# A decode attention and gated-MLP kernel: each V tile by one transfer of 128 partitions in place of four of 32

## The chip, the cores and the metric

The kernel runs on one core of one Trainium2 chip. The metric is the device time of one execution in microseconds (us). Three runs of the kernel before gave 198.82, 197.82 and 198.64 us, a median of 198.64 us. The profile comes from one more execution, which took 197.94 us.

A core has five engines that run their own instruction streams: PE (TensorE, matmul), DVE (VectorE), ACT (ScalarE), POOL (GpSimd) and SP (SyncE). Data comes from device memory (HBM) into the on-chip memory (SBUF, 128 partitions) by DMA transfers. A transfer is issued from the stream of SP, ACT or POOL; the profile counts 16 DMA engines that move the bytes, whichever stream issued it.

## The reference, cut to what matters

One decode step for 8 sequences (batch B = 8, one query each), 32 query heads over 8 key/value heads, a head size of 128, and a window of the last 2048 of 8192 cached keys. Beside the attention stands a gated MLP whose output, after a SiLU, multiplies the attention output.

```python
xn = layernorm(x)                                        # x: [8, 1, 512]
q  = (xn @ wq)                                           # wq: [512, 4096] -> 32 heads of 128
k, v = k_cache[:, :, Sk-W:, :], v_cache[:, :, Sk-W:, :]  # [8, 8, 2048, 128] of [8, 8, 8192, 128]
p  = softmax(q k^T / sqrt(128));  s = (p v) @ wo         # four query heads share a key/value head
h  = sigmoid(xn @ w_gate) * (xn @ w_up)                  # [512, 1792] each
g  = silu(h @ w_down)                                    # [1792, 512]
out = x + s * g
```

All inputs and the output are bf16. The bytes read are 33.6 MB of K, 33.6 MB of V and about 14 MB of weights.

## The kernel before, in words

Everything large goes through a ring of five SBUF buffers (`RING = 5`, `ring_tile` in line 109). The order of the tiles is: `wq`, eight K tiles, eight V tiles (one for each sequence), gate and up weights, down weights, and `wo`. A tile may be loaded as soon as the tile five places before it has been used up; `issue_loads` (line 190) issues what is allowed at each step of the main loop. `wq` and K are issued on SP's queue, V and the later weights on POOL's (`load_v` in line 137, `load_gate_up`, `load_down` and `load_wo` in lines 153 to 179). Every large transfer's instruction has line 107.

A K tile is 4 MB: 32 pairs of (sequence, head) outside, four runs of 128 keys inside, so 128 partitions of 32 KB each, in one transfer. A V tile is also 4 MB: one sequence, eight heads, 16 runs of 128 consecutive keys, again 128 partitions of 32 KB. Before the change it comes in four transfers of 1 MB. Transfer `s` fills partitions 32s to 32s+31 with four of the 16 runs; inside it the eight heads stand outside and the four runs inside, so partition 32s + 4h + i holds head h, run 4s + i. They are issued in the order `V_ORDER = (0, 2, 1, 3)`: partitions 0 to 31, 64 to 95, 32 to 63, 96 to 127.

The work is a software pipeline written out by hand. The main loop (line 620) has 122 steps. Step t turns one eighth of a K tile on DVE (`k_turn`, line 437), multiplies an earlier one with the queries on PE (`qk`, line 452), and from step 58 on also multiplies an eighth of a V tile with the probabilities (`pv`, line 570). A K tile counts as used up after its last `qk`, a V tile after its last `pv`. The sequences come in two halves of four (`hb`); for each half the softmax follows its fourth K tile: row maximum (`soft_max_part`, line 466), exponentials on ACT (`soft_exp`, line 480), 32x32 turns on DVE (`soft_turn`, line 500), and then `soft_spread` (line 513).

`soft_spread` multiplies the turned probabilities by a constant matrix of zeros and ones, `spread`, so that each probability lands in the partition that holds its keys in the V tile. `soft_mask` (line 532) then multiplies by `Hm`, which is one where a partition holds head h and zero elsewhere, so that one matmul over 128 partitions serves all eight heads. Both constants are made once, from the identity matrix: `Hm` by one reduction on DVE (line 278), `spread` by a memset and four copies on POOL (lines 286 and 291). They hold the order of the partitions in the V tile.

After the last V tile follow the MLP (`unit_in`, `unit_mid`, `unit_out`), the output projection with `wo` (line 666, in six pieces so that the last one is small), and two small stores.

Of the kernel before, what the change touches and what calls it, by code (L numbers as in the profile page):

```python
# [10 lines left out]
def kernel(  # L11
# [13 lines left out]
    nc = tc.nc  # L25
    P = 128
    B, _, D = A_x.shape
    _, Hkv, Sk, Dh = A_k_cache.shape
# [6 lines left out]
    win0 = Sk - W  # L35
# [7 lines left out]
    PP = P // Hkv  # L43
    CH = W // PP
# [23 lines left out]
    CB = CH // 4  # L68
    NCH = 2
    RING = 5  # L70
    VI = 32 // Hkv
    VS = PP // VI
    V_ORDER = (0, 2, 1, 3)
    NCOL = 2
    DC = D // NCOL

    bf16 = mybir.dt.bfloat16
    f32 = mybir.dt.float32
    AF = mybir.ActivationFunctionType
    ALU = mybir.AluOpType  # L80
    AX = mybir.AxisListType
# [3 lines left out]
    consts = ctx.enter_context(tc.tile_pool(name="consts", bufs=1))  # L85
# [18 lines left out]
    def load(dst, src, q=None):  # L104
        if q is None:
            q = nc.sync
        q.dma_start(out=dst, in_=src)  # L107

    def ring_tile(shape, name):
        return ring.tile(shape, bf16, name=name, tag="ring", align_bytes=ALIGN)  # L110

    x_bf = work.tile([B, D], bf16, name="x_bf")
    for c in range(4):
        nc.scalar.dma_start(
            out=x_bf[:, P * c : P * (c + 1)],
            in_=A_x.flatten_outer_dims()[:, P * c : P * (c + 1)],
# [19 lines left out]

    def load_v(b):
        t = ring_tile([P, CH, Dh], "v_sb")
        for s in V_ORDER:
            k0 = win0 + VI * CH * s  # L140
            load(
                t[32 * s : 32 * (s + 1)].rearrange("p c d -> p (c d)"),
                A_v_cache[b, :, k0 : k0 + VI * CH, :].rearrange(
                    "h (i c) d -> h i (c d)", c=CH
                ),
                nc.gpsimd,
            )
        v_tiles[b] = t

    wgu_sb = []  # L150
# [39 lines left out]
    def issue_loads():  # L190
        while loads_done[0] < len(loads):
            x = loads[loads_done[0]]
            kind, i = x
            at = order.index(x)
            if at >= RING and order[at - RING] not in released:
                break
            if kind == 0:
                load_k(i)
            elif kind == 1:
                load_v(i)  # L200
            else:
                (load_gate_up, load_down, load_wo)[i]()
            loads_done[0] += 1

    issue_loads()
    ident = consts.tile([P, P], bf16, name="ident")
# [19 lines left out]
        out=rstd[:], in_=mv[:, 1:2], func=AF.Sqrt, bias=eps_t[:], scale=1.0  # L226
# [4 lines left out]
        out=xn_bf[:],  # L231
# [7 lines left out]
    for kt in range(KT):  # L239
        nc.tensor.transpose(  # L240
            out=xnT_ps[:, kt, :], in_=xn_bf[:B, kt::KT], identity=ident[:B, :B]
        )
    x2_ps = psum1.tile([NCOL * 32, DC], f32, name="x2_ps", tag="misc")
    for c in range(NCOL):
        nc.tensor.matmul(
            x2_ps[32 * c : 32 * (c + 1), :],
            lhsT=ident[:B, :32],
# [15 lines left out]
        out=HR[:],  # L263
        in_=ident[:].rearrange("m (h q r) -> m h r q", q=NQ, r=rep),
        axis=AX.X,
# [5 lines left out]
        out=Qm[:],  # L271
        in_=ident[:].rearrange("m (h q r) -> m q h r", q=NQ, r=rep),
        axis=AX.XY,
# [3 lines left out]
    Hm = consts.tile([P, Hkv], f32, name="Hm")  # L277
    nc.vector.tensor_reduce(
        out=Hm[:],
        in_=ident[:].rearrange("p (s h i) -> p h s i", s=VS, h=Hkv),  # L280
        axis=AX.XY,
        op=ALU.add,
    )

    spread = consts.tile([P, 2, 2, VS, Hkv // 2, 2, VI], bf16, name="spread")
    nc.gpsimd.memset(
        spread[:].rearrange("p o y s b e i -> p (o y s b e i)").bitcast(f32), 0.0
    )
    for o in range(2):
        for y in range(2):  # L290
            nc.gpsimd.tensor_copy(
                out=spread[:, o, y, :, :, y, :],
                in_=ident[:].rearrange(
                    "p (b s i o) -> p o s b i", s=VS, i=VI, o=2
                )[:, o],
            )

    w = NCH * Hq
# [2 lines left out]
        out=rows_of[:],  # L301
        in_=ident[:].rearrange("p (a m) -> p m a", m=w),
        axis=AX.X,
# [4 lines left out]
        out=Sel[:], in_=rows_of[:].rearrange("p (h c r) -> p c h r", c=NCH, r=rep)  # L308
# [195 lines left out]
    def soft_spread(hb):  # L504

        pt = pt_of.pop(hb)[:].rearrange("p c (y m) -> p c y m", y=2)
        pc = ppool.tile([P, NQ, 2, CH // 2, rep], bf16, name="pc_bf", tag="pp")
        for o in range(2):
            for ch in range(2):
                c = slice(CB * ch, CB * (ch + 1))  # L510
                pT_ps = psum_a.tile([P, CB, NQ, rep], f32, name="pT_ps", tag="acc_ps")
                for y in range(2):
                    nc.tensor.matmul(  # L513
                        pT_ps[:],
                        lhsT=spread[:, o, y].rearrange("p s b e i -> p (s b e i)"),
                        rhs=pt[:, c, y, :],
                        start=(y == 0),
                        stop=(y == 1),
                        skip_group_check=True,
                    )  # L520
                nc.scalar.copy(  # L521
                    out=pc[:, :, o, c, :].rearrange("p q c r -> p c q r"),
                    in_=pT_ps[:],
                )
        pc_of[hb] = pc
# [94 lines left out]
    for t in range(PV_LAG + NSLOT):  # L620
# [22 lines left out]
        for hb in range(HB):  # L643
            if t == EXP_AT[hb] + SPREAD_LAG:
                soft_spread(hb)
            if t == EXP_AT[hb] + 5:
                soft_den(hb)
# [16 lines left out]
    for k in range(KW):  # L664
        for c in range(NCOL):
            nc.tensor.matmul(  # L666
                a_ps[32 * c : 32 * (c + 1), :],
                lhsT=o2_sb[:, k, :],
# [11 lines left out]
    for c in range(NCOL):  # L680
        queues[c].dma_start(
            out=out.flatten_outer_dims()[:, DC * c : DC * (c + 1)],
            in_=y_bf[32 * c : 32 * c + B, :],
# [31 lines left out]
```

## Time and profile before

| what | value |
|---|---|
| runs before | 197.82 to 198.82 us, median 198.64 |
| the profiled execution | 197.94 us |
| its span, first to last instruction | 196.1 us |
| moved by DMA | 81.19 MB, mean 414 GB/s over the span |
| DVE busy | 114.5 us (58%) |
| PE busy | 95.0 us (48%) |
| POOL busy, ACT busy | 25.5 us (13%), 24.6 us (13%) |
| V transfers | 32 of 1024 KB on POOL's queue, 19.5 us each from issue to landing (median) |
| K transfers | 8 of 4096 KB on SP's queue, 41.7 us (median) |

The span is 1.8 us shorter than the time of the same execution; the rest lies before the first and after the last instruction. The profile's page first gives each engine's busy time, then the span in 40 slices of 4.9 us, with the busy share of the DMA engines in tenths and the GB/s that they moved, then the DMA queues, then the chain of work that ended last, then groups of instructions with their idle time and what released them.

### The profile page before, as it was taken

The numbers are of one execution on the slowest core, as the hardware profiler recorded it, in microseconds if no ns is written. First come the engines' busy times: TensorE is split into PE (matmuls) and PEld (weight loads), VectorE is DVE, ScalarE is ACT, GpSimd is POOL, SyncE is SP. The second block draws the span as 40 slices with busy tenths as digits, with TensorE's granted clock in tenths as the row PEclk, the third lists the DMA queues.
The fourth block names the chain that finished last, engine by engine and source line by source line (L and its number), as shares of the span: only waits on it lengthen the run. The fifth ranks groups of instructions, "written<-read, shape, count | busy, mean of one in ns | idle before, by whom it ended". The sixth has DMA issues, their size and how long they took to land.

```text
span 196.1 us, 2425 instructions
## 1 busy us (share of the span) xinstructions
PE 95.0 (48%) x986; PEld 52.4 (27%) x986; DVE 114.5 (58%) x196; ACT 24.6 (13%) x61; POOL 25.5 (13%) x58
## 2 busy tenths in 40 slices
PE   0008014434323248432252896698292929285483
PEld 0002001111001012100021345187272727271361
DVE  0025799999899999979959944555313130010501
ACT  2002450000000083000000005311000000031000
POOL 7000000000000400402112222222222122210000
PEclk9999999999999999955555589699879796997579
DMA  6999999999999999999999999999999999999990
GB/s 214 429 428 448 435 461 448 430 435 438 421 428 428 435 428 428 428 425 428 428 435 428 428 428 425 428 430 425 448 418 435 430 430 431 401 433 432 420 387 34
DMA packets 5004, 81.19 MB, mean 414 GB/s; under 512 B 1904, under 2 KB 1920, under 8 KB 2176
## 3 DMA queue, kind: packets, MB, share of 16 engines
q0 software_dynamic: 3600, 43.26, 51.8%
q1 hardware_dynamic: 1312, 37.75, 45.0%
q8 instruction: 8, 0.13, 0.2%
q14 instruction: 4, 0.03, 0.0%
q10 hardware_dynamic: 80, 0.01, 0.0%
HBM read 81.01 MB, written 0.01 MB: 413 GB/s over the span
## 4 chain that ended last, share of the span: by engine, by line
DMA 68%; DVE 22%; PE 6%; ACT 1%; issue 1%; POOL 0%; SPq 0%; POOLq 0%; ACTq 0%
DMA k_sb<-in_A_k_cache_dram 35%; DMA v_sb<-in_A_v_cache_dram 20%; DVE k_sb L437 16%; DMA wo_sb<-in_A_wo_dram 13%; PE s_ps L452 2%; PE acc_ps L570 2%; DVE pT_sb L532 2%; ACT p_bf L480 1%; DVE pt_bf L500 1%; DVE mx L466 1%; PE a_ps L666 1%; PE pT_ps L513 1%; DVE qz_sb L408 0%; DVE qT_sb L398 0%; POOL wo_sb L107 0%
## 5 line engine op out<-in xcount | busy, mean ns | idle before, releaser
L437 DVE STREAM_TRANSPOSE k_sb<-k_sb 128x1024 f32<-128x1024 f32 x64 | 73.7, 1208 | 5.3 <-DMA k_sb<-in_A_k_cache_dram 5.3
L452 PE MATMUL s_ps<-k_sb,qz_sb 128*32 128x512 bf16 x256 | 30.2, 591 | 55.5 <-DVE k_sb L437 49.7
L570 PE MATMUL acc_ps<-v_sb,pT_sb 128*64 128x256 bf16 x512 | 38.0, 304 | 16.5 <-DMA v_sb<-in_A_v_cache_dram 16.5
L570 PEld LDWEIGHTS <-pT_sb 128*64 128x64 bf16 x512 | 29.5, 122 | 25.4 <-issue 24.2
L107 POOL DMA_DIRECT2D v_sb<-in_A_v_cache_dram x32 | 17.2, 542 | 130.0 <-PE s_ps L452 80.0
L452 PEld LDWEIGHTS <-qz_sb 128*32 128x32 bf16 x256 | 8.7, 120 | 76.2 <-issue 49.9
L532 DVE TENSOR_SCALAR pT_sb<-pc_bf,Hm 128x512 bf16<-128x512 bf16 x64 | 17.5, 345 | 12.5 <-PE acc_ps L570 12.5
L594 DVE TENSOR_SCALAR o_sb<-o_ps,rden 32x128 bf16<-32x128 f32 x8 | 2.7, 336 | 24.8 <-PE o_ps L587 24.8
L581 ACT COPY acc_sb<-acc_ps 128x256 f32<-128x256 f32 x8 | 3.0, 372 | 81.7 <-PE acc_ps L570 81.7
L513 PE MATMUL pT_ps<-pt_bf,spread 128*128 128x512 bf16 x16 | 7.1, 595 | 4.2 <-DVE pt_bf L500 3.6
L217 DVE CAST x_f<-x_bf 8x512 f32<-8x512 bf16 x1 | 0.4, 416 | 13.1 <-DMA x_bf<-in_A_x_dram 13.1
L240 PE MATMUL xnT_ps<-ident,xn_bf 8*128 8x8 bf16 x4 | 0.3, 175 | 15.6 <-DVE xn_bf L230 15.6
L500 DVE STREAM_TRANSPOSE pt_bf<-p_bf 128x512 bf16<-128x512 bf16 x8 | 4.9, 674 | 2.7 <-ACT p_bf L480 2.7
L480 ACT ACT_TABLE_LOAD x1 | 1.3, 1283 | 39.9 <-DVE nm L474 39.9
L587 PE MATMUL o_ps<-acc_sb,Sel 128*32 128x128 f32 x32 | 6.3, 331 | 0.0
L480 ACT ACTIVATE p_bf<-s_ps,nm 128x512 bf16<-128x512 f32 x8 | 5.4, 685 | 2.9 <-DVE nm L474 2.9
L521 ACT CAST pc_bf<-pT_ps 128x512 bf16<-128x512 f32 x8 | 4.7, 585 | 7.4 <-PE pT_ps L513 4.7
L410 ACT COPY qz_sb<-qT_sb 32x32 bf16<-32x32 bf16 x20 | 4.8, 241 | 4.7 <-DVE qT_sb L398 4.4
L666 PE MATMUL a_ps<-wo_sb,o_sb 128*32 128x256 bf16 x64 | 5.0, 299 | 0.7 <-DMA wo_sb<-in_A_wo_dram 0.7
L466 DVE TENSOR_REDUCE mx<-s_ps 128x1 f32<-128x512 f32 x8 | 5.2, 653 | 0.0
L107 POOL DMA_DIRECT2D wo_sb<-in_A_wo_dram x6 | 3.2, 535 | 10.5 <-DMA v_sb<-in_A_v_cache_dram 7.4
L352 PE MATMUL b_ps<-wd_sb,hT_sb 128*32 128x256 bf16 x28 | 3.2, 418 | 2.8 <-DVE hT_sb L344 2.8
(63 smaller groups left out, 48.0 us busy)
## 6 DMA issues: line engine op xcount, KB each, us to landing
k_sb<-in_A_k_cache_dram SPq DMA_DIRECT2D x8, 4096.0 KB, 41.7
v_sb<-in_A_v_cache_dram POOLq DMA_DIRECT2D x32, 1024.0 KB, 19.5
wq_sb<-in_A_wq_dram SPq DMA_DIRECT2D x1, 4096.0 KB, 12.4
wo_sb<-in_A_wo_dram POOLq DMA_DIRECT2D x1, 2048.0 KB, 26.2
wgu_sb<-in_B_w_gate_dram POOLq DMA_DIRECT2D x1, 1792.0 KB, 18.3
wgu_sb<-in_B_w_up_dram POOLq DMA_DIRECT2D x1, 1792.0 KB, 22.0
wd_sb<-in_B_w_down_dram POOLq DMA_DIRECT2D x1, 1792.0 KB, 21.9
wo_sb<-in_A_wo_dram POOLq DMA_DIRECT2D x1, 1024.0 KB, 24.6
```

Of the source, the lines that this page charges most:

```text
L107: q.dma_start(out=dst, in_=src)
L410: nc.scalar.copy(out=out, in_=in_)
L437: nc.vector.transpose(out=kw, in_=kw)
L452: nc.tensor.matmul(s_tiles[i][32 * g : 32 * (g + 1), :], lhsT=qz_sb[:, hb, h, 2 * a + e, :], rhs=kT[:, :, a, h, :, e], start=(n == 0), sto ...
L466: nc.vector.reduce_max(out=mx_of[hb][:, kq : kq + 1], in_=s_tiles[i][:], axis=AX.X)
L480: nc.scalar.activation(out=p_bf[:, :, kq], in_=s_tiles.pop(NK * hb + kq)[:].rearrange("p (o c j) -> p c j o", o=2, j=NC), func=AF.Exp, bia ...
L500: nc.vector.transpose(out=pt[:, w * n : w * (n + 1)], in_=p_bf[:, w * n : w * (n + 1)])
L513: nc.tensor.matmul(pT_ps[:], lhsT=spread[:, o, y].rearrange("p s b e i -> p (s b e i)"), rhs=pt[:, c, y, :], start=(y == 0), stop=(y == 1) ...
L532: nc.vector.tensor_scalar(out=pT_of[b][:, :, h, :], in0=pc, scalar1=Hm[:, h : h + 1], scalar2=None, op0=ALU.mult,)
L570: nc.tensor.matmul(acc_tiles[b][w * c : w * (c + 1), :], lhsT=pT_of[b][:, ch // NCH].rearrange("p h n -> p (h n)"), rhs=v_tiles[b][:, ch : ...
L587: nc.tensor.matmul(o_ps[:], lhsT=Sel[:, c].rearrange("p h r -> p (h r)"), rhs=acc_sb[:, Dh * c : Dh * (c + 1)], start=(c == 0), stop=(c == ...
L666: nc.tensor.matmul(a_ps[32 * c : 32 * (c + 1), :], lhsT=o2_sb[:, k, :], rhs=wo_parts[k][:, DC * c : DC * (c + 1)], start=(k == 0), stop=(k ...
```

## The change

`load_v` issues one transfer of 4 MB over all 128 partitions in place of four over 32. On the side of the device memory the 16 runs of keys are now outside and the eight heads inside, so partition 8p + h holds head h, run p. The bytes are the same, and so is the size of the piece that a partition receives (32 KB). Since the partitions are in another order, `Hm` and `spread` are built from the identity matrix with another view; their sizes and the matmuls that use them keep their shapes. `V_ORDER`, `VI` and `VS` fall away.

```diff
     def load_v(b):
         t = ring_tile([P, CH, Dh], "v_sb")
-        for s in V_ORDER:
-            k0 = win0 + VI * CH * s
-            load(
-                t[32 * s : 32 * (s + 1)].rearrange("p c d -> p (c d)"),
-                A_v_cache[b, :, k0 : k0 + VI * CH, :].rearrange(
-                    "h (i c) d -> h i (c d)", c=CH
-                ),
-                nc.gpsimd,
-            )
+        load(
+            t[:].rearrange("p c d -> p (c d)"),
+            A_v_cache[b, :, win0:Sk, :].rearrange("h (p c) d -> p h (c d)", c=CH),
+            nc.gpsimd,
+        )
         v_tiles[b] = t
...
     nc.vector.tensor_reduce(
         out=Hm[:],
-        in_=ident[:].rearrange("p (s h i) -> p h s i", s=VS, h=Hkv),
-        axis=AX.XY,
+        in_=ident[:].rearrange("p (k h) -> p h k", h=Hkv),
+        axis=AX.X,
         op=ALU.add,
     )
 
-    spread = consts.tile([P, 2, 2, VS, Hkv // 2, 2, VI], bf16, name="spread")
+    spread = consts.tile([P, 2, 2, PP, Hkv // 2, 2], bf16, name="spread")
...
             nc.gpsimd.tensor_copy(
-                out=spread[:, o, y, :, :, y, :],
-                in_=ident[:].rearrange(
-                    "p (b s i o) -> p o s b i", s=VS, i=VI, o=2
-                )[:, o],
+                out=spread[:, o, y, :, :, y],
+                in_=ident[:].rearrange("p (b k o) -> p o k b", k=PP, o=2)[:, o],
             )
...
-                        lhsT=spread[:, o, y].rearrange("p s b e i -> p (s b e i)"),
+                        lhsT=spread[:, o, y].rearrange("p k b e -> p (k b e)"),
```

More of the change, by code (lines that the diff above doesn't have):

```diff
@@ L70 @@
     RING = 5
-    VI = 32 // Hkv
-    VS = PP // VI
-    V_ORDER = (0, 2, 1, 3)
     NCOL = 2
@@ L279 @@
         out=Hm[:],
-        in_=ident[:].rearrange("p (s h i) -> p h s i", s=VS, h=Hkv),
-        axis=AX.XY,
+        in_=ident[:].rearrange("p (k h) -> p h k", h=Hkv),
+        axis=AX.X,
         op=ALU.add,
     )
-    spread = consts.tile([P, 2, 2, VS, Hkv // 2, 2, VI], bf16, name="spread")
+    spread = consts.tile([P, 2, 2, PP, Hkv // 2, 2], bf16, name="spread")
     nc.gpsimd.memset(
-        spread[:].rearrange("p o y s b e i -> p (o y s b e i)").bitcast(f32), 0.0
+        spread[:].rearrange("p o y k b e -> p (o y k b e)").bitcast(f32), 0.0
     )
```

## The prediction

> **What bounds the kernel now.** I read the page's slices first, since they show where in the span an engine is full, then the queues, then the stretches by stage, and last POOL's timeline, because the change touches POOL's issues.
>
> ```profile
> DMA  6999999999999999999999999999999999999990
> GB/s 214 429 428 448 435 461 448 430 435 438 421 428 428 435 428 428 428 425 428 428 435 428 428 428 425 428 430 425 448 418 435 430 430 431 401 433 432 420 387 34
> q0 software_dynamic: 3600, 43.26, 51.8%
> q1 hardware_dynamic: 1312, 37.75, 45.0%
> DMA 68%; DVE 22%; PE 6%; ACT 1%; issue 1%; POOL 0%; SPq 0%; POOLq 0%; ACTq 0%
> ```
>
> All 16 DMA engines are full from the second slice to the last but one, and the two queues together fill 96.8% of the span. The time is a start of some 2 us, 81 MB at about 430 GB/s, and a tail of some 4 us. No engine's work sets it: the chain's DVE share lies inside transfers that are under way at the same time.
>
> ```profile
> 10.00:60.00 50.00, 17.45 (x150) 5.57 (x151) 42.23 (x61) 6.66 (x24) 0.00 (x0) 1.00 1.01 435
> 102.00:162.00 60.00, 40.28 (x467) 26.93 (x463) 29.94 (x80) 7.34 (x18) 13.03 (x25) 0.81 1.01 431
> ```
>
> The last two columns are the DMA share and GB/s. In the first stretch almost only K moves, in the second only V: 435 against 431 GB/s. V is already carried at K's rate within 1%.
>
> ```profile
> 110.86 0.53 POOL L107 DMA_DIRECT2D v_sb<-in_A_v_cache_dram  x1 [3.41 <-DMA v_sb<-in_A_v_cache_dram]
> 111.72 0.53 POOL L107 DMA_DIRECT2D v_sb<-in_A_v_cache_dram  x1 [0.33 <-DMA v_sb<-in_A_v_cache_dram]
> ...
> 120.58 0.53 POOL L107 DMA_DIRECT2D v_sb<-in_A_v_cache_dram  x1 [3.12 <-DMA v_sb<-in_A_v_cache_dram]
> 121.46 0.53 POOL L107 DMA_DIRECT2D v_sb<-in_A_v_cache_dram  x1 [0.35 <-DMA v_sb<-in_A_v_cache_dram]
> ```
>
> These issues wait for an earlier V transfer to land, so their times tell landings. Two land 0.86 us apart, and the same place of the next tile comes 9.7 us later (4 MB at 431 GB/s). Transfers that each used all 16 engines in turn would land 2.4 us apart. So two are carried side by side, each at half the rate: a V transfer with eight heads outermost is dealt to eight engines, a head to each. The issue order makes the pairs partitions 0 to 31 with 64 to 95, and 32 to 63 with 96 to 127. An engine writes four neighbouring partitions.
>
> **The change, part by part.** The sum is made on the profiled execution, 197.94 us; the median of the three runs is 0.70 us above it.
>
> *POOL's issues.* 32 by 542 ns become 8: 13.0 us of POOL go. POOL is 13% busy and ahead of the queue, which is never empty, so this is 0. Without that cover it would be 0.54 us for each transfer that an engine waits for.
>
> *Waits of the issues.* V issues sat idle 54.4 us in 18 waits for earlier V transfers. With eight transfers in all these waits go and an issue waits for its buffer only. Queued behind them on POOL are the five issues of gate, up, down and the first `wo` piece, and the smaller pieces; they come some us earlier but their bytes stand behind V's in the same full queue: 0. SP's issues are not passed. If the queue ran dry, each of the idle times (up to 5.8 us) would count, and it does not.
>
> *Completion records.* Queue 0 takes 51.8% of 16 x 196.1 us for 43.26 MB, 37.57 us of one engine per MB; queue 1 45.0% for 37.75 MB, 37.40. The difference over 43.26 MB is 7.2 engine-us, 0.45 us of time: all that queue 0's 41 transfers cost beyond bytes. 24 of the 41 go: 0.26 us gained (ends: 0 and 0.45).
>
> *Constants.* `Hm` is one reduction of 280 ns at 16.4 us, first used at 92.7; the four copies of `spread` take 233 ns each at 2.5 us, first used at 73.7. Doubled by other strides they cost DVE 0.28 us, where DVE then idles 1.62 us before `qT_sb`, and POOL 0.9 us, where POOL then idles until 65 us: 0, and halved 0 as well. The matmuls of line 513 and the masks of line 532 keep their shapes: 0.
>
> *The rows themselves.* This is the term that decides. A row of 32 KB takes an engine 37.57 us/MB x 0.0328 MB = 1.23 us; an engine carries 8 rows of each V tile, 64 in all, 78.7 us. Dealt by the outermost dimension again, the new transfer goes to 16 engines, one run of keys to each with its eight heads. That is eight neighbouring partitions in place of two groups of four. So engines p and p+4 write partitions 32 apart at the same moment, which the pairs of before never do. No row shows what two such writes do to each other. One end is 0: K, also 128 partitions in one transfer of 32 KB rows, loses nothing at 435 GB/s, but it is dealt 32 pieces of four partitions. The other end is that both share one way into SBUF and a row takes 2.46 us: 64 x 1.23 = 78.7 us more. K's row is the nearest in size, but not in the grouping, which is what changes; V and K, two queues and two layouts, sit at one rate per engine within 1%, which looks like a limit on each engine's own path, with nothing spare for a second writer. I take the upper end, less a little: each pair starts up to a row out of step, which takes a part of four rows out of the collision; the unluckiest of eight pairs sets the landing, and I give it a fifth of a row in four, 5%. 64 x 1.23 x 0.95 = 74.8 us. A gain is bounded below, by the rate of K.
>
> Sum: 197.94 - 0.26 + 74.8 = 272.5 us.
>
> [...]
>
> **The rivals.**
>
> *No collision, same time.* The two writes do not hinder each other, or the dealing keeps four neighbouring partitions to an engine as it does for K. For it: K at 435 GB/s from one transfer over 128 partitions. Against it: 16 pieces cannot be dealt as 32. The time is 197.94 - 0.26 = 197.7 us, 197.2 to 198.6 with the runs' scatter.
>
> *Half a collision.* The pairs fall out of step, for K's rows stand between V's until about 102 us and records of instruction code stop single engines. At two rows out of step half of the 78.7 us is left: 197.7 + 39.3 = 237 us. Against it: nothing shifts a pair by four rows (4.9 us), and a pair in step stays so.
>
> *Faster.* V reaches K's rate and the records go: 33.55 MB at 431 GB/s are 77.8 us, at 435 77.1, so 197.94 - 0.7 - 0.26 = 197.0 us, just under the half per cent. It decides from 436 GB/s in the V stage upward. Against it: no stretch of 50 us is above 435, and the engines have no gap to close.
>
> [...]
>
> **How the numbers follow.** Collision nearly in full: 0.45. Half a collision or less, over 199 us: 0.15. No collision: 0.37. Faster: 0.03. The likeliest is the first, 272.5 us, with a range of its own from 255 (one row in four out of step: 197.7 + 59) to 276.4 (full). The range must reach the third case, which holds more than 2 in 10: 197.2 to 276.5 us. About half a per cent, 1 us, is what a measurement of this kernel can tell from no change. Slower 0.60, same 0.37, faster 0.03.
>
> **What would show it.** Right: the slices' GB/s fall toward 220 to 300 from about 65 us on while the DMA share stays full, K's later tiles land late as well (their rows alternate with V's on the engines), queue 0's share of the engines rises although its MB stay, and PE's idle time before line 570, 16.5 us for V now, grows by tens of us. POOL shows 8 V issues, none waiting for V to land. Gate, up and down stay at their rate. Wrong: GB/s stay at 430 in the V stage; then the time is the second rival's, and eight neighbouring partitions cost nothing. A fall of the rate with no rise of queue 0's share would mean a queue run dry, not a collision.

## The result: half as long again

The changed kernel takes 300.1 us (median of four runs, 297.3 to 306.18) against 198.58 us before. The ratio is 1.5075, with an interval of 1.4925 to 1.5226; it leaves out the run of 306.18 us, which lies 3% above the shortest. The profiled execution is that longest run; its span is 304.2 us. The forecast was 272.5 us, 197.2 to 276.5: the direction was right, the size outside the range.

The page of the changed kernel, slices (DMA share in tenths, GB/s), packet counts and queues:

```profile
DMA  8999999999999999999999999999999999999992
GB/s 319 436 418 431 461 415 416 440 448 224 194 198 183 194 207 198 207 215 211 220 224 215 207 215 222 208 205 211 211 209 211 207 212 207 224 193 315 431 415 95
DMA packets 3594, 81.16 MB, mean 267 GB/s; under 512 B 496, under 2 KB 512, under 8 KB 768
q0 software_dynamic: 2192, 43.25, 61.2%
q1 hardware_dynamic: 1312, 37.75, 36.4%
```

A slice is now 7.6 us. From the tenth slice (68 us, where the first V rows start) to the 36th the rate is half of what it was, while the engines stay full. The engines don't wait; each row takes longer, 2.5 us in the median of V's in place of 1.21. The last slices, where only weights are left, are back at 415 to 431 GB/s.

Stretches of the changed kernel (the last two columns are DMA share and GB/s): K alone, K and V together in two parts, V alone.

```profile
10.00:60.00 50.00, 17.41 (x150) 5.53 (x151) 42.17 (x61) 6.64 (x24) 0.00 (x0) 1.00 1.01 434
70.00:110.00 40.00, 11.73 (x74) 3.23 (x73) 15.77 (x19) 5.20 (x13) 1.04 (x2) 1.00 1.01 192
110.00:160.00 50.00, 5.90 (x48) 2.08 (x48) 11.83 (x17) 0.00 (x0) 0.51 (x1) 1.00 1.00 214
165.00:270.00 105.00, 45.40 (x498) 31.51 (x498) 30.64 (x81) 7.73 (x19) 6.04 (x11) 0.76 1.01 212
```

V alone runs at 212 GB/s against 431 before, a factor of 2.03. But K and V together run no faster, at 192 and then 214: K's rows, whose layout has not changed, are slowed too while V's stand beside them. The trace keeps one record for each DMA packet, and a row of 32 KB is one packet. A K row that starts before the first V row, at 69 us, takes 1.21 us in the median. From there until K is through, at 163 us, it takes 2.5. V's rows take 2.5 us where they are alone.

The queues say what each part costs. Queue 1 (K, `wq`) takes 36.4% of 16 x 304.2 us, 1772 engine-us for 37.75 MB, where it took 45.0% of 16 x 196.1, 1412: 360 more, 22.5 us on each of 16 engines. Queue 0 (V and the later weights) takes 2979 engine-us in place of 1625: 84.6 us on each engine. Together 107.1 us; the two profiled executions differ by 306.18 - 197.94 = 108.2 us. So the whole loss is time in which an engine moves a row, and a fifth of it is K's in this longest run. If V costs the three shorter runs the same, some 14 to 19 us are left in them for K, an estimate; the kernel four8 below, 297.13 us, pays 84.6 us for V and 14.4 for K.

PE's wait for V grows from 16.5 to 57.0 us, and DVE waits 69.9 us for K tiles, 5.3 before. POOL's eight V issues keep their price. Two groups of the kernel before, and then three of the changed kernel:

```profile
L437 DVE STREAM_TRANSPOSE k_sb<-k_sb 128x1024 f32<-128x1024 f32 x64 | 73.7, 1208 | 5.3 <-DMA k_sb<-in_A_k_cache_dram 5.3
L570 PE MATMUL acc_ps<-v_sb,pT_sb 128*64 128x256 bf16 x512 | 38.0, 304 | 16.5 <-DMA v_sb<-in_A_v_cache_dram 16.5
```

```profile
L428 DVE STREAM_TRANSPOSE k_sb<-k_sb 128x1024 f32<-128x1024 f32 x64 | 73.7, 1209 | 70.0 <-DMA k_sb<-in_A_k_cache_dram 69.9
L561 PE MATMUL acc_ps<-v_sb,pT_sb 128*64 128x256 bf16 x512 | 43.2, 332 | 57.0 <-DMA v_sb<-in_A_v_cache_dram 57.0
L104 POOL DMA_DIRECT2D v_sb<-in_A_v_cache_dram x8 | 4.5, 564 | 189.2 <-PE s_ps L443 137.4
```

### The profile page after: what moved, and what is told of

The parts are those of the page before. It is cut to its first block, busy times and chain, and to the rows that moved or that the text cites. A ratio compares the mean times of both kernels' runs of the same rounds, so it can differ in the third digit from the quotient of the medians.

```text
span 304.2 us, 2389 instructions
## 1 busy us (share of the span) xinstructions
PE 99.6 (33%) x986; PEld 55.5 (18%) x986; DVE 114.8 (38%) x196; ACT 24.6 (8%) x61; POOL 13.1 (4%) x34
## 3 DMA queue, kind: packets, MB, share of 16 engines
q1 hardware_dynamic: 1312, 37.75, 36.4%
## 4 chain that ended last, share of the span: by engine, by line
DMA 36%; another core or an unknown queue 24%; issue 14%; PE 13%; DVE 12%; POOL 0%; SPq 0%; POOLq 0%
DMA k_sb<-in_A_k_cache_dram 23%; DMA v_sb<-in_A_v_cache_dram 12%; DVE k_sb L428 9%; PE acc_ps L561 8%; PE a_ps L657 1%; PE o_ps L578 1%; PE b_ps L343 1%; DVE pT_sb L523 1%; PE s_ps L443 1%; PE d_ps L317 1%; DVE o_sb L606 0%; DVE mx L457 0%; DVE hT_sb L335 0%; DVE qz_sb L399 0%
## 5 line engine op out<-in xcount | busy, mean ns | idle before, releaser
L428 DVE STREAM_TRANSPOSE k_sb<-k_sb 128x1024 f32<-128x1024 f32 x64 | 73.7, 1209 | 70.0 <-DMA k_sb<-in_A_k_cache_dram 69.9
L443 PE MATMUL s_ps<-k_sb,qz_sb 128*32 128x512 bf16 x256 | 31.3, 606 | 111.2 <-DVE k_sb L428 105.4
L561 PE MATMUL acc_ps<-v_sb,pT_sb 128*64 128x256 bf16 x512 | 43.2, 332 | 57.0 <-DMA v_sb<-in_A_v_cache_dram 57.0
L561 PEld LDWEIGHTS <-pT_sb 128*64 128x64 bf16 x512 | 33.1, 134 | 67.1 <-issue 65.0
L104 POOL DMA_DIRECT2D v_sb<-in_A_v_cache_dram x8 | 4.5, 564 | 189.2 <-PE s_ps L443 137.4
L657 PEld LDWEIGHTS <-o_sb 128*32 128x32 bf16 x64 | 3.6, 97 | 3.6 <-issue 3.4
## 6 DMA issues: line engine op xcount, KB each, us to landing
wgu_sb<-in_B_w_gate_dram POOLq DMA_DIRECT2D x1, 1792.0 KB, 78.7
```

Source lines behind the costliest of these rows:

```text
L428: nc.vector.transpose(out=kw, in_=kw)
L443: nc.tensor.matmul(s_tiles[i][32 * g : 32 * (g + 1), :], lhsT=qz_sb[:, hb, h, 2 * a + e, :], rhs=kT[:, :, a, h, :, e], start=(n == 0), sto ...
L561: nc.tensor.matmul(acc_tiles[b][w * c : w * (c + 1), :], lhsT=pT_of[b][:, ch // NCH].rearrange("p h n -> p (h n)"), rhs=v_tiles[b][:, ch : ...
L657: nc.tensor.matmul(a_ps[32 * c : 32 * (c + 1), :], lhsT=o2_sb[:, k, :], rhs=wo_parts[k][:, DC * c : DC * (c + 1)], start=(k == 0), stop=(k ...
```

## The experiments

Three theories were set against each other. A: two engines that write partitions 32 apart at the same time share one way into SBUF. B: the reads are slower, since each engine walks through eight heads 2 MB apart. C: one transfer of 4 MB on POOL's queue is carried more slowly than four of 1 MB. The packet records give queue, size and times, but neither the engine nor the partitions of a row; that an engine carries neighbouring partitions, and that two engines share a way in, is the author's assumption in A, tried here by what follows from it. Two more questions came up: where the time beyond V's own rows comes from, and what the number of transfers does by itself.

### Only the order of the four transfers (order0123)

```diff
 # the kernel before
-    V_ORDER = (0, 2, 1, 3)
+    V_ORDER = (0, 1, 2, 3)
```

> The kernel before, with its four V transfers of 32 partitions issued in the order 0, 1, 2, 3 in place of 0, 2, 1, 3; sizes, source rows, constants and the number of transfers stay. Theory A (two engines that write partitions 32 apart at the same time share one way into SBUF): partitions 0 to 31 are now carried beside 32 to 63, and 64 to 95 beside 96 to 127, so V goes at some 212 GB/s as in the changed kernel, and the time is 290 to 310 us. Theory B (the reads are slower: each engine walks through eight heads that lie 2 MB apart): the reads are those of before, 198 us. Theory C (one transfer of 4 MB on POOL's queue is carried more slowly than four of 1 MB): four transfers, 198 us.

Measured: 282.62 us, ratio 1.427 (1.4226 to 1.4314). The page of this kernel:

```profile
GB/s 299 448 447 415 405 444 445 447 424 410 359 298 296 224 289 373 224 224 214 193 191 225 219 217 219 196 196 219 221 219 214 200 197 220 212 194 422 428 406 52
q0 software_dynamic: 3600, 43.26, 63.5%
q1 hardware_dynamic: 1312, 37.75, 33.9%
```

Every transfer, read and constant is that of before; only which two transfers are under way together has changed, and V falls to the same 190 to 225 GB/s (212 from 120 to 220 us). The rows that are read and the sizes of the transfers stay, so B and C, as they stand, can't give it; A foretold it. The time lies below the expected 290 to 310. By the queues, V's side costs 77.0 us more (2858 against 1625 engine-us) and K's 7.1 (1526 against 1412), together 84.1 of the measured 84.6 us. K pays less here than in the changed kernel: while K and V go together, the slices stand at 224 to 410 GB/s, not at 200. This would follow if the pairs met only part of the time in this stretch, which no view shows directly.

### Another order that keeps the blocks apart (order0312)

```diff
 # the kernel before
-    V_ORDER = (0, 2, 1, 3)
+    V_ORDER = (0, 3, 1, 2)
```

> The kernel before with its four transfers in the order 0, 3, 1, 2: partitions 0 to 31 beside 96 to 127, then 32 to 63 beside 64 to 95. Theory A: no two blocks that lie 32 apart inside one half of the partitions are carried side by side, so nothing is lost: 197.5 to 199 us. If any order but 0, 2, 1, 3 is slow, or if blocks that lie 96 or 32 apart across the halves meet as well: 240 to 290 us.

Measured: 197.96 us against 198.03, ratio 0.9994 (0.9977 to 1.001). So it isn't that 0, 2, 1, 3 alone is good: blocks 0 and 3 as well as 1 and 2 pass side by side without loss. Of the pairs tried, only 0 with 1 and 2 with 3 collide, those that lie 32 apart inside one half of the partitions; 1 and 2 are 32 apart as well, but across the halves. This run also rules out that transfers collide because they read neighbouring stretches of memory: blocks 1 and 2 lie 128 KB apart in each head, just as 0 and 1 do, and lose nothing.

### The changed layout by four transfers (four8)

```diff
 # the changed kernel
-        load(
-            t[:].rearrange("p c d -> p (c d)"),
-            A_v_cache[b, :, win0:Sk, :].rearrange("h (p c) d -> p h (c d)", c=CH),
-            nc.gpsimd,
-        )
+        for s in (0, 2, 1, 3):
+            k0 = win0 + 4 * CH * s
+            load(
+                t[32 * s : 32 * (s + 1)].rearrange("p c d -> p (c d)"),
+                A_v_cache[b, :, k0 : k0 + 4 * CH, :].rearrange(
+                    "h (p c) d -> p h (c d)", c=CH
+                ),
+                nc.gpsimd,
+            )
```

> The changed kernel's layout (16 runs outside, eight heads inside, its constants) loaded by four transfers of 32 partitions in the order 0, 2, 1, 3, each with four runs outside and eight heads inside. Theory A: dealt by the outermost dimension, four engines carry a transfer, eight neighbouring partitions to each, and the four transfers run side by side on 16 engines, so partitions 32 apart are again written at the same time: 290 to 310 us. Theory B: the reads are those of the changed kernel, 300 us. Theory C: four transfers of 1 MB, 198 us.

Measured: 297.13 us, ratio 1.5002 (1.4965 to 1.504), as A says and against C: with the runs outside and the heads inside, 32 transfers of 1 MB are as slow as eight of 4 MB (297.3 to 301.68 us in the three shorter runs). By the queues V's side costs 84.6 us more on each engine than before (2978 against 1625 engine-us) and K's 14.4 (1643 against 1412), together 99.0 of the measured 99.1 us. The page of this kernel, with its count of small packets:

```profile
DMA packets 7052, 81.20 MB, mean 275 GB/s; under 512 B 3952, under 2 KB 3968, under 8 KB 4224
q0 software_dynamic: 5648, 43.27, 63.1%
q1 hardware_dynamic: 1312, 37.75, 34.8%
```

Under 512 B there are 496 packets in the changed kernel, 1904 before, 3952 here. In the changed kernel 272 packets of 4 bytes stand in queue 0 for its 17 transfers, 16 for each. Before has 24 transfers more: 24 x 16 are 384, and 1024 are left, 32 for each of its 32 V transfers. Here 3072 are left, 96 for each. Eight engines without a row times four rows is 32, twelve times eight is 96: the counts fit a V transfer that goes to eight engines with four rows each before, to four engines with eight rows each here, and to all 16 in the changed kernel. This is the author's reading. No record names the engine of a packet, no run shows why an engine without a row would be given small packets, and the count does not say which partitions an engine writes; it was used below to foretell another kernel's count.

### One transfer with K's source (one32x4)

```diff
 # the changed kernel
+        hb, kq = divmod(b, NK)
+        k0 = win0 + NC * KC * kq
-            A_v_cache[b, :, win0:Sk, :].rearrange("h (p c) d -> p h (c d)", c=CH),
+            A_v_cache[NQ * hb : NQ * (hb + 1), :, k0 : k0 + NC * KC, :].rearrange(
+                "b h (j c) d -> (b h) j (c d)", c=KC
+            ),
```

> The changed kernel with one transfer of 4 MB for each V tile on POOL's queue, but its source is read as a K tile's is: 32 pairs of sequence and head outside, four runs of keys inside. The tile then holds a quarter of the window of four sequences, so the probabilities meet other values than they belong to; the bytes, the number of transfers and all other work stay. Theory A: 32 pieces of four partitions, two pieces to an engine, partitions 32 apart on the same engine one after the other: no two writers meet, 197.5 to 199 us. Theory B: an engine reads two stretches of 128 KB in place of eight of 32 KB: 198 us. Theory C: still one transfer of 4 MB on POOL's queue: 300 us.

Measured: 200.97 us, ratio 1.0154 (1.0124 to 1.0184). One transfer of 128 partitions on POOL's queue is not slow: C falls, and with order0123 the reads as the whole cause are out as well. That rows 32 apart are here on one engine is A's assumption and not shown; the run shows only that this source doesn't collide (435 GB/s from 70 to 100 us). And 2.9 us are lost that theory A does not explain. Stretches of this kernel and then of the kernel before (last two columns as above):

```profile
70.00:100.00 30.00, 10.99 (x78) 3.19 (x79) 20.06 (x24) 4.80 (x12) 1.06 (x2) 0.56 1.01 435
120.00:140.00 20.00, 15.56 (x156) 7.92 (x156) 12.56 (x25) 5.22 (x13) 1.09 (x2) 0.78 0.95 394
```

```profile
70.00:100.00 30.00, 13.12 (x98) 4.00 (x101) 27.34 (x36) 5.08 (x12) 3.73 (x7) 0.72 1.01 435
120.00:140.00 20.00, 13.29 (x168) 9.33 (x164) 9.90 (x33) 5.65 (x15) 4.24 (x8) 0.91 1.01 432
```

Between 70 and 100 us both move 435 GB/s, but here DVE turns 20 us of K in place of 27: K gets less of the engines. Between 120 and 140 us the engines are no longer full: 20 x (432 - 394) / 432 = 1.8 us are missing. DVE waits for the last K tile until 114.6 us, where K's last transfer had landed by 101.7 before. So buffers come free later: POOL's timeline has the fourth V issue at 110.51 us, released by `qk` (L447), and the fifth only at 128.82, released by `pv` (L565), which takes turns with the late `qk` on PE.

```profile
110.51 0.53 POOL L104 DMA_DIRECT2D v_sb<-in_A_v_cache_dram  x1 [21.21 <-PE s_ps L447]
128.82 0.53 POOL L104 DMA_DIRECT2D v_sb<-in_A_v_cache_dram  x1 [17.78 <-PE acc_ps L565]
```

### The same source by four transfers (four32x4)

```diff
 # one32x4
-        load(
-            t[:].rearrange("p c d -> p (c d)"),
-            A_v_cache[NQ * hb : NQ * (hb + 1), :, k0 : k0 + NC * KC, :].rearrange(
-                "b h (j c) d -> (b h) j (c d)", c=KC
-            ),
-            nc.gpsimd,
-        )
+        v_src = A_v_cache[NQ * hb : NQ * (hb + 1), :, k0 : k0 + NC * KC, :].rearrange(
+            "b h (j c) d -> b h j (c d)", c=KC
+        )
+        for s in (0, 2, 1, 3):
+            load(t[32 * s : 32 * (s + 1)].rearrange("p c d -> p (c d)"), v_src[s], nc.gpsimd)
```

> As one32x4 (source read as a K tile's, so the tile holds other values than the probabilities belong to), but by four transfers of 32 partitions, one for each of four sequences, in the order 0, 2, 1, 3. It tells where the 3 us of one32x4 come from. If they come from the number of transfers (eight of 4 MB may be under way in place of eight of 1 MB, so V takes half the engines' time from 65 us on in place of 37%, K lands later and frees buffers later, and the queue runs dry for a moment): 198 us. If they come from the source or from the constants: 201 us.

Measured: 197.89 us, ratio 1.0 (0.9984 to 1.0017). With the source and the constants of one32x4 the 2.9 us are gone, so they belong to the number of transfers. Between 120 and 140 us the engines are full again:

```profile
120.00:140.00 20.00, 12.75 (x158) 8.86 (x154) 9.89 (x33) 5.02 (x13) 4.39 (x9) 0.91 1.02 435
```

The expected reason, a limit on the transfers under way, does not fit: by the issue times and the packet records V never has more than 8.0 MB under way in the kernel before, and no more than 8.4 MB in one32x4 until 130 us. What differs is how the packets of the two queues are shared out. These are the packets that ended between 80 and 95 us, while K and V go together:

| kernel | queue 1 (K) | queue 0 (V) | of these, V rows of 32 KB | of these, packets of 4 bytes |
|---|---|---|---|---|
| before | 156 | 158 | 63 | 95 |
| four32x4 | 156 | 156 | 63 | 93 |
| four8 | 106 | 104 | 25 | 79 |
| one32x4 | 126 | 112 | 96 | 16 |

In each of the four kernels the two queues have about as many packets carried as each other (104 to 158 in the 15 us), whatever a packet holds. A packet of 4 bytes takes 9 ns and a row 1.21 us in the kernel before, but in these counts each is one. By this count the small packets of four transfers hold V back: it gets 63 of 203 rows before, 96 of 206 in one32x4. There K lands later, its buffers come free later, and the queue runs dry for a moment. No run changes the small packets alone, so this cause is argued from the counts.

### V behind K in one queue (one_sp)

```diff
 # the changed kernel, load_v
-            nc.gpsimd,
+            nc.sync,
```

> The changed kernel with V's transfers on SP's queue, behind K's in the same queue. It tells what the 26 us are by which the changed kernel is slower than V's own rows explain. If K's rows pay for standing beside V's (both at 2.5 us in 65 to 165 us): here K is through before V starts, K's rows stay at 1.21 us, only V's 64 rows per engine pay 1.27 us each, 81 us, and the time is 275 to 284 us. If V's rows themselves cost more than double or the rest is POOL's queue: 300 us, or 198 us where the whole loss belongs to POOL's queue.

Measured: 305.57 us, ratio 1.5429 (1.5375 to 1.5482). The time is not the expected 275 to 284 us, and by itself it would speak for the other case, rows of V that cost more than double. The queues of this page tell otherwise.

```profile
q1 hardware_dynamic: 2464, 71.31, 81.9%
q0 software_dynamic: 1040, 9.70, 12.5%
```

Queue 1 now has K, V and `wq`. At before's 37.40 us per MB its 71.31 MB would be 2667 engine-us; it takes 0.819 x 16 x 303.0 = 3971, so 81.5 us more on each engine, 1.27 us for each of the 64 V rows. That is all of V's doubling and nothing for K, which was through at full rate (413 to 467 GB/s in the second to the twelfth slice). But the weights, alone on POOL's queue, now stand beside V in place of behind it: 606 engine-us for 9.70 MB against 364 at 37.57 us per MB, 15 us on each engine. What is left of the 107.5 us, 11 us, lies at the end: the last two slices, from 288 us on, stand at 10 and 3 GB/s, and PE still has the rest of the MLP and the output projection to do. The collision is also the same on SP's queue: 212 GB/s from 165 to 270 us.

### Half of the tiles, after K is through (last4)

```diff
 # the changed kernel, load_v
+        if b >= 4:
             load(
                 t[:].rearrange("p c d -> p (c d)"),
                 A_v_cache[b, :, win0:Sk, :].rearrange("h (p c) d -> p h (c d)", c=CH),
                 nc.gpsimd,
             )
+        else:
+            for s in (0, 2, 1, 3):
+                k0 = win0 + 4 * CH * s
+                load(
+                    t[32 * s : 32 * (s + 1)].rearrange("p c d -> p (c d)"),
+                    A_v_cache[b, :, k0 : k0 + 4 * CH, :].rearrange(
+                        "h (i c) d -> h i (c d)", c=CH
+                    ),
+                    nc.gpsimd,
+                )
```

> The first four V tiles by four transfers in the layout of before, the last four by one transfer each as in the changed kernel; the constants are those of the changed kernel, so the first four sequences meet their V rows in another order. If every row that stands beside colliding rows pays, and nothing else does: K is through before the colliding tiles start, they cost 4 x 8 rows x 1.27 us = 41 us, and the time is 237 to 243 us, far less than half of the changed kernel's 102 us. If each V tile costs the same wherever it stands: 198 + 51 = 249 us.

Measured: 239.7 us, ratio 1.2097 (1.2057 to 1.2138), in the middle of the expected 237 to 243. The page of this kernel:

```profile
GB/s 265 443 441 441 441 436 426 408 428 425 436 436 442 442 433 436 431 408 419 433 436 366 229 199 204 237 201 221 204 221 217 204 232 196 201 306 434 426 409 59
q0 software_dynamic: 2896, 43.26, 60.1%
q1 hardware_dynamic: 1312, 37.75, 37.2%
```

Queue 1 takes 0.372 x 16 x 237.5 = 1414 engine-us, the 1412 of before: K pays nothing when it doesn't stand beside colliding V rows. Queue 0 pays 41.2 us on each engine, 32 rows at 1.29 us. The first four tiles of the changed kernel therefore carry about 60 of its 102 us: their own 41 us and K's share.

### Heads outside in one transfer (heads_out)

```diff
 # the changed kernel; Hm and spread to match
-            A_v_cache[b, :, win0:Sk, :].rearrange("h (p c) d -> p h (c d)", c=CH),
+            A_v_cache[b, :, win0:Sk, :].rearrange("h (p c) d -> h p (c d)", c=CH),
```

> One transfer of 4 MB for each V tile on POOL's queue as in the changed kernel, but with the eight heads outside and the 16 runs inside; constants to match. Dealt by the outermost dimension it goes to eight engines, 16 neighbouring partitions to each, and the next tile goes to the other eight beside it. [...] If it only mattered that an engine's partitions are many or that two engines meet: a row of 2.5 us as in the changed kernel, 290 to 310 us. The page should count 1520 packets under 512 B.

Measured: 424.55 us (416.2 and 432.91). The page of this kernel:

```profile
GB/s 355 412 449 425 432 452 358 203 203 204 253 237 168 190 146 104 114 100 127 111 108 104 108 101 125 108 114 111 114 117 104 115 105 123 101 114 100 342 423 157
DMA packets 4619, 81.16 MB, mean 196 GB/s; under 512 B 1521, under 2 KB 1537, under 8 KB 1793
q0 software_dynamic: 3216, 43.26, 72.0%
```

In V's own stretch the slices stand at 100 to 127 GB/s, about a quarter of 431; by the packet records V's rows take 4.8 us from 175 us on. By the expected dealing engines h and h+2 of a tile write 32 apart, and beside them the same two of the next tile: four writers, which is the author's reading. If four hinder each other as two do, that is 4 x 1.21 = 4.9 us a row, an estimate from the row of the kernel before, and with it 33.55 MB in 311 us in place of 78, some 431 us in all. The two runs lie at 416.2 and 432.91 us. The row of 2.5 us and the 290 to 310 us, where it only matters that two engines meet, did not come. Theory B would not give it: with the heads outside the 16 rows of a head are one unbroken stretch of memory, and yet this kernel is the slowest of all. The small packets are 1521 where 1520 were foretold, which by the reading of four8 is eight engines with 16 rows each. Between 100 and 125 us, beside K, V's rows take 2.4 us, so the four do not hinder each other in full from the start. Why they do not no run shows.

## Why the prediction was right in direction and wrong in size

*What bounds the kernel* held: the DMA engines are full from end to end in both, and the whole change of time is in the engines' time per row. No term of PE, DVE, ACT or POOL mattered.

*The rows themselves* was the right step: two writers of partitions 32 apart at the same time, inside one half of the partitions as order0312 has it. order0123 and order0312 show the collision with nothing but the order changed (282.62 and 197.96 us), and the rows of heads_out, 4.8 us in place of 2.5, fit one that goes by the number of writers. The packet counts fit the dealing by the outermost dimension, as far as the number of engines goes; which partitions an engine writes, and what two writers share, no run shows. That a row beside another writer takes twice its time was the author's choice between two ends, with no row of before to show it; the changed kernel showed it, with 2.5 us a row and 212 GB/s for V alone. The signs came as the prediction named them, only stronger: 183 to 224 GB/s where it had 220 to 300.

Its size was wrong in two places. The first: V's rows were priced at 78.7 us less 5% for pairs out of step. No discount was due: V alone falls from 431 to 212 GB/s, a little more than half, and queue 0 pays 84.6 us, more than the 78.7 taken as the upper end. That alone makes the sum 282.3 us, above the range. A head start of a part of a row bought nothing that the queue shares show.

The second is the larger, and is the step that failed. The sum let V's rows pay for the collision and nobody else. K's rows stand between them on the same engines, and in the 94 us in which both are under way a K row takes twice its time as well: 22.5 us on each engine in the profiled execution, 14.4 in four8, which the sum did not have. Why a K row is slowed is open: it may meet V's writers itself, or wait behind the V row of its own engine; the records show only how long it takes. The text did expect K's tiles to land late, but only because their rows alternate with V's, and so at no price. last4, where K is through before, has no such term; one_sp has it on the weights in place of K. With 84.6 and 22.5 in place of 74.8 the sum would be 304.8 us, against 306.18 of the profiled execution; with four8's 84.6 and 14.4 it would be 296.7, against 296.74 of four8's profiled execution.

*Waits of the issues*, costed at nothing: no run shows that they cost anything. One transfer in place of four does cost 2.9 us where nothing collides, 1.5% (one32x4; four32x4 loses none of it). The packet counts point to the term *Completion records*, which priced the small packets by their time, 0.45 us at most, and not by their number. 1408 of them are gone in the changed kernel: 16 for each of 24 transfers, 384, and 1024 more, 32 for each V transfer of before. What they are for no run shows.

*POOL's issues* (542 and 564 ns) and the *constants* cost what was said: nothing that shows. four32x4 has the changed kernel's constants and takes 197.89 us.

The rival of half a collision, 237 us, did not come to pass; that of no collision is what one32x4 shows for another source (435 GB/s from 70 to 100 us, 200.97 us in all).

Three slips of the prediction's text change nothing in the sum. The 54.4 us in 18 waits are 37.9 us in 13 waits of V issues and 16.5 us in 5 waits of PE's matmuls. Gate, up, down and the first `wo` piece are four issues, not five. And 197.7 + 59 is 256.7 us, not 255.

## What to carry to other kernels

When the DMA engines bound a kernel, look at which partitions are written at the same time, not only at whether the engines are full: in these kernels the order of the source's dimensions, or of four issues, decided between 431 and 212 GB/s for V with 16 full engines. Price a collision on everything that shares the engines in that stretch, not on the colliding transfer alone. And count packets as well as bytes: in these counts packets that take 9 ns each stood for as much as rows of 1.21 us when two queues went together, so the same stretch is to be read again when they go.

## What the runs showed that was not expected

- 43% more time by the order of four issues alone: 282.62 us in the order 0, 1, 2, 3, 197.96 and 198.03 us in 0, 3, 1, 2 and 0, 2, 1, 3.
- Rows whose own layout has not changed take twice as long beside such as collide: K rows 2.5 us in place of 1.21.
- Two queues got about as many packets carried as each other (156 and 158 before, 126 and 112 in one32x4, from 80 to 95 us), so by the counts 4-byte packets held V back in favour of K: 31% of the rows before, 47% with one transfer for each tile.
- The page's share of busy DMA engines doesn't show the loss: apart from the ends it reads 9 in every slice, at 212 GB/s as at 431.
